# Moving three pieces of hand-ordered work in an attention and feed-forward kernel: key differences, output products, first row maxima

## The chip, the cores and the metric

The kernel runs on one core of a Trainium2 chip. The metric is the device time of one execution in microseconds; lower is better. The profile is one execution, taken by the hardware profiler; its engines are PE (matrix multiply; PEld is its weight load), DVE (VectorE), ACT (ScalarE), POOL (GpSimd) and SP (SyncE, which here only issues transfers).

## The reference

A transformer block on one sequence of 2048 rows of 576 numbers: a layer norm, attention with 32 heads of 18 numbers, an output product with a residual, a second layer norm, and a gated feed-forward part with 4608 inner columns.

```python
x = A_x                                                   # 1 x 2048 x 576
h = x + _A_ref(_layernorm(x), A_wqkv, A_wo)
h2 = h + _B_ref(_layernorm(h), B_w_gate, B_w_up, B_w_down)

def _A_ref(x, wqkv, wo):                                  # 32 heads, Dh = 18
    q, k, v = split(x @ wqkv)
    p = softmax(einsum("bhqd,bhkd->bhqk", q, k) * Dh ** -0.5)
    return einsum("bhqk,bhkd->bhqd", p, v) @ wo

def _B_ref(x, w_gate, w_up, w_down):
    return (gelu(x @ w_gate) * (x @ w_up)) @ w_down
```

## The kernel before

Products of float32 precision are made from pairs of float16 numbers (a high and a low part), so every product is three matmuls.

**Stages.** First come the layer norm and the products for q, k and v; then the attention loop; then the feed-forward part.

**The attention loop** runs over 32 blocks `n`. A block is one group of four heads (`g = n // 4`) and 512 queries (`qc = n % 4`), and walks over 16 key tiles `kt` of 128 keys. For each key tile PE makes four score tiles of 128 keys by 512 queries (`score`, line 670), ACT takes their exponentials (line 672), and PE weighs the values with them (`weigh`, line 679, one key tile later).

**Row maxima run ahead.** Before a block's scores can be made, the largest score of each query must be known; it is subtracted inside the score product, as two extra rows of the stacked queries. PE makes the scores once more for this (`max_bank`, line 618) and DVE reduces each bank (line 629), 64 banks to a block, some 1.45 blocks ahead: 93 banks are made before the loop, eight for every two key tiles in it. `max_finish` ends a block: DVE takes the last maximum (line 638), POOL splits it into float16 parts (lines 641 to 643), SP turns them (`mT`, line 645) and issues four transfers that put them into the stacked queries (line 651, tiles `A` or `W`). So the last maximum is made in block 30, key tile 8.

**Key differences.** A quarter of the banks for maxima use differences of neighbouring key stretches in place of keys. `load_ends` (line 591) loads keys, `key_steps` has POOL subtract them (lines 598 to 601), and SP writes them to DRAM (`kd`, line 604) and reads them back (line 606). It is done once for each group of heads after the first, a group ahead: in block 1 and in blocks 4, 8, 12, 16, 20 and 24.

**Out-block.** When a block has been weighed, `out_block` works in three steps in the next block: the sums are taken from the banks, added on POOL (line 696), and their denominators fetched (`rc`, line 701); the reciprocals are made on POOL (lines 708 to 712; on DVE, line 714, for the last four blocks) and spread over the partitions through DRAM (lines 716 and 717); and `o` is scaled (line 721 on POOL, 725 on DVE for the last two), split, and written into the stack `X` (lines 736 to 740).

**Output product.** `wo_block(b)` multiplies four row tiles of `o` by `wo` (PE line 301, 14 matmuls to a half tile; eight half tiles to a block of rows), adds the residual (DVE line 809), and takes the statistics of the second layer norm; POOL makes their roots in pairs of tiles (`rstd_beside`, line 226 on). Rows of block `b` need `o` of all heads, that is, of the last group. `rows0` then norms the first 1024 rows in pairs (tile `i` and tile `4 + i`), makes sums of them on POOL (lines 850 to 853) and float16 parts on DVE (lines 859 to 863), and SP turns them into the layout of the feed-forward products (line 889). The feed-forward part begins when PE comes to line 1135.

**What sets the order.** PE, ACT, DVE and POOL execute what the code issues, in that order. Inside the attention loop the order on SP is chosen by the scheduler, which may move a transfer ahead of others whose data are later; every engine and queue then works strictly in its order. `take(it)` advances a piece of work by one step, and the steps of a key tile stand in `STEPS`: `s` a score tile, `m` a bank for maxima, `w` half a key tile weighed, `f` other work, where `side` is the splitting of the first weights on POOL.

Of the kernel before, what the change touches and what calls it, by code (L numbers as in the profile page):

```python
# [26 lines left out]
HALF = D // 2  # L27
# [5 lines left out]
def tile_block(  # L33
# [18 lines left out]
    nc = tc.nc  # L52
# [4 lines left out]
    NT = S // P  # L57
    TB = min(512, S)
    NB = S // TB
    TPB = TB // P  # L60
# [5 lines left out]
    NG = H // 4  # L66
# [13 lines left out]
    def ring(items):  # L80
        while True:
            yield from items

    p_ring = ring(quads)
    m_ring = ring(singles)
    

    nat = const.tile([P, NT, D], F32, name="nat")
# [97 lines left out]
    def row_stats(src, t):  # L186
        st = small.tile([P, 2, 6], F32, tag="st", name="st", bufs=4)
        for i in range(2):
            nc.vector.bn_stats(st[:, i], src[:, i * HALF : (i + 1) * HALF])
        nc.vector.bn_aggr(mv[:, t], st)  # L190
# [26 lines left out]
    minus_half = const.tile([P, 1], F32, name="minus_half")  # L217
    nc.gpsimd.memset(minus_half, -0.5)

    def rstd_beside(t0, nt, scale):  # L220

        sl = slice(t0, t0 + nt)
        v = small.tile([P, nt], F32, tag="ln_v", name="ln_v")
        r = small.tile([P, nt], F32, tag="ln_r", name="ln_r")
        u = small.tile([P, nt], F32, tag="ln_u", name="ln_u")
        nc.gpsimd.tensor_scalar_add(v, mv[:, sl, 1], EPS)
        nc.gpsimd.tensor_tensor(r, v, minus_half.to_broadcast([P, nt]), op=ALU.pow)
        for k in (1.0, scale):
            nc.gpsimd.tensor_mul(u, r, r)
            nc.gpsimd.tensor_mul(u, u, v)  # L230
            nc.gpsimd.tensor_scalar(u, u, -0.5 * k, 1.5 * k, op0=ALU.mult, op1=ALU.add)
            nc.gpsimd.tensor_mul(r if k == 1.0 else rs[:, sl], u, r)
        nc.gpsimd.tensor_mul(u, mv[:, sl, 0], rs[:, sl])
        nc.gpsimd.tensor_scalar_mul(nb[:, sl], u, -1.0)
# [79 lines left out]
    def take(it, n=1):  # L314
        for _ in range(n):
            next(it, None)
# [4 lines left out]
    xv = x.rearrange("(t p) d -> p t d", p=P)  # L321
# [422 lines left out]
    NS = NG * NB  # L744
    UPS = TPB * NB
    AHEAD = UPS + 8 * UPS // 16
# [19 lines left out]
    u_o = const.tile([P, 1], F32, name="u_o")  # L766
# [25 lines left out]
    xbs = [view(A, MAT, (D,)), view(WK, 19968, (D,))]  # L792
    PIECES = 2 * NK + 9

    def wo_block(b, ring_, xbs=xbs):

        def fetch(t):
            if t < (b + 1) * TPB:
                nc.sync.dma_start(xbs[t % 2], xv[:, t])

        fetch(b * TPB)
        fetch(b * TPB + 1)
        yield
        for t in range(b * TPB, (b + 1) * TPB):
            for i in range(2):
                ws = slice(i * HALF, (i + 1) * HALF)
                pt = next(ring_)
                run(accumulate(pt[:, :HALF], products(slice(t * P, (t + 1) * P), oh, ol, ws)))
                nc.vector.scalar_tensor_tensor(nat[:, t, ws], pt[:, :HALF], u_o, xbs[t % 2][:, ws],
                                               op0=ALU.mult, op1=ALU.add)  # L810
                yield
            fetch(t + 2)
            row_stats(nat[:, t], t)
            if t % 2:
                rstd_beside(t - 1, 2, 256.0)
        yield


    VP = view(V, 0, (2 * PIECES, TB), F16)
# [10 lines left out]
    def rows0():  # L830

        o = 2 * PIECES * TB
        parts = [(view(r, k, (4, 5 * P), F16), view(V, o + 8064 + 5120, (2, 5 * P), F16),
                  view(V, o + 8064 + 7680, (1, 5 * P), F16))
                 for r, k in ((V, o + 8064), (tmp3.rearrange("p a b -> p (a b)"), 0))]
        r12 = view(V, o + 8064 + 5120, (3, 5 * P), F16)
        bufs = [(view(V, o, (7, HALF)), T4s),
                (view(nat1, 18432, (7, HALF)), view(nat1, 18432 + 4 * 7 * HALF, (HALF,)))]
        M2, M3 = 2 * P, 3 * P
        for rows in (parts[0][0], parts[1][0], r12):  # L840
            nc.gpsimd.memset(rows[:, :, M3 - KR : M3], 0.0)

        def sums(i):
            F, T4 = bufs[i % 2]
            b12, B22, B11, B21, T1, T2, T3 = (F[:, k] for k in range(7))
            y2, y1 = (F.rearrange("p a b -> p (a b)")[:, k * D : (k + 1) * D] for k in range(2))
            normed(y1, nat[:, i], i)
            normed(y2, nat[:, TPB + i], TPB + i)
            yield
            nc.gpsimd.tensor_sub(T1, b12, B11)  # L850
            nc.gpsimd.tensor_sub(T2, B22, T1)
            nc.gpsimd.tensor_sub(T4, B21, T2)
            nc.gpsimd.tensor_sub(T3, B22, b12)
            yield

        def cut_rows(i):
            F, T4 = bufs[i % 2]
            for k, (f, r) in enumerate(zip((F[:, 1:5], F[:, 5:7], T4.unsqueeze(1)), parts[i % 2])):
                nc.vector.tensor_copy(r[:, :, :HALF], f)
                yield  # L860
                nc.vector.tensor_sub(r[:, :, M3:], f[:, :, :M2], r[:, :, :M2])
                nc.vector.tensor_sub(r[:, :, HALF : HALF + KR], f[:, :, M2:], r[:, :, M2:HALF])
                nc.vector.tensor_copy(r[:, :, HALF + KR : HALF + 2 * KR], r[:, :, M2:HALF])
                if k == 0:
                    turn_rows(0, i, 0, 20, r)
                elif k == 2:
                    turn_rows(0, i, 20, 35, r12)
                yield

        yield from sums(0)  # L870
        for i in range(TPB):
            if i + 1 < TPB:
                yield from sums(i + 1)
            yield from cut_rows(i)
# [63 lines left out]
    B22, B11, B21, T1, T2, T3, T4 = range(7)  # L938
# [306 lines left out]
    mxs = maxima()  # L1245
# [9 lines left out]
    fill = other_products()  # L1255
    side = iter(())
    take(fill, 18)
    for i in range(5 * AHEAD // 4):
        take(mxs, 1 if i == 5 * AHEAD // 4 - 1 else 3 + (i % 5 == 4))
        if i == AHEAD // 4:  # L1260
            raw_loads()
        if i >= AHEAD // 3:
            take(sums)
        take(fill, 2 + (i % 5 == 2))
    run(sums)
    m_ring = ring(singles[:3] + quads[:3])
    accs = (singles[3], quads[3])
    STEPS = ("smsmwsmsf", "wsmssmmwsmmwf")
    halves = deque([None, None])
    for n in range(NS):  # L1270
        g, qc = divmod(n, NB)
        late = n > NS - NB
        for kt in range(NT):
            heads = iter(range(4))
            for step in STEPS[kt % 2]:
                if step == "s":
                    score(n, kt, next(heads))
                elif step == "m":
                    take(mxs)
                elif step == "w":  # L1280
                    half_ = halves.popleft()
                    if half_ is not None:
                        weigh(*half_)
                        if half_[1] == NT - 1 and half_[3] == 1:
                            ob = out_block(half_[0], accs)
                            next(ob)
                else:
                    if n < NS - 1 or kt < 11:
                        take(fill, 2)
                    take(side)  # L1290
            halves += [(n, kt, accs, q) for q in range(2)]
            if n and kt in ((2 if n == NS - 1 else 4, 7) if late else (4, 6)):
                take(ob)
            if late and kt == 11:
                run(fill)
                fill = wo_block(qc - 1, m_ring)
                take(fill, qc == 3)
            if n == NS - 2 and kt == NT - 1:
                rows = rows0()
            if n * NT + kt >= (NS - 1) * NT - 1:  # L1300
                take(rows, 2)
            if g == 0 and qc == 0 and kt == NT - 1:
                run(fill)
                init_set(sets[1])
            if g + 1 < NG and kt == 2 and qc == (1 if g == 0 and NB > 1 else 0):
                load_stacks(g + 1)
                load_ends(g + 1)
            if g + 1 < NG and kt == 8 and qc == (1 if g == 0 and NB > 1 else 0):
                key_steps(g + 1)
            if n == 2 and kt == 4:  # L1310
                side = prepare_wo()
            if n == NS - NB and kt == 2:
                blank_rows()
                load_matrix(w_gate, 0, nc.gpsimd)
            if n == NS - NB and kt == 8:
                side = chain(split_early(0, 0, lambda: load_matrix(w_up, 0, nc.gpsimd)), pause(2),
                             split_early(0, 1, lambda: load_matrix(w_gate, 1, nc.gpsimd)),
                             pause(2), until_ready(second))
# [18 lines left out]
    m_ring = ring([singles[3], more[3]])  # L1337
# [27 lines left out]
    rows = chain(rows1(), first_load())  # L1365
# [63 lines left out]
```

## Time and profile before

| | |
|---|---|
| median of 3 runs | 2678.67 us (2677.91 to 2679.49) |
| profiled execution | 2680.21 us |
| its span | 2678.4 us |
| PE busy | 2591.2 us (97%) |
| DVE busy | 2003.9 us (75%) |
| ACT busy | 1666.6 us (62%) |
| POOL busy | 856.7 us (32%) |
| mean granted PE clock | 0.985 |
| attention loop, about | 204 to 1455 us |
| feed-forward part, from | 1469.66 us |

The busy shares are means over stages with different limits. In the attention loop ACT, DVE and PE are all nearly full; in the feed-forward part PE alone is. Times of rows are microseconds from the start of the span. A row of the timeline has start, duration, engine, line and operation, and in brackets how long the engine was idle before it and what ended that. A row of the waits has the total, the number of waits, and the longest.

### The profile page before, as it was taken

What the parts mean: (1) busy time and instruction counts of PE and PEld (TensorE: products, weight loads), DVE (VectorE), ACT (ScalarE), POOL (GpSimd) and SP (SyncE); (2) the same over time, 40 slices, a digit from 0 to 9 for tenths busy, and PEclk for the clock granted to TensorE, in tenths of its full rate; (3) what the DMA queues carried; (4) which work ended last, traced back from release to release, by engine and by line L of the source; (5) the groups of instructions that cost most, each with busy time, mean ns of one, the idle gap of its engine ahead of it and who ended that gap; (6) DMA issues with size and microseconds to landing.
All of it is one profiled execution on the core that took longest, in us unless ns stands there. A gap on an engine that the chain in (4) does not pass through costs nothing.

```text
span 2678.4 us, 96899 instructions
## 1 busy us (share of the span) xinstructions
PE 2591.2 (97%) x41245; PEld 1495.0 (56%) x41245; DVE 2003.9 (75%) x3888; ACT 1666.6 (62%) x3154; POOL 856.7 (32%) x1176
## 2 busy tenths in 40 slices
PE   8999899989998999999989999999999999999999
PEld 4545555555555555555555555555555555555555
DVE  7479889989898999989856766565656566666653
ACT  6229889989898999989955533333333333333332
POOL 4302532322323232332755632222222222222221
PEclk9999999999999999999989999999999999999999
DMA  8621010101101010100115331010101010101010
GB/s 221 149 83 39 18 48 19 42 18 32 35 18 42 18 47 20 42 17 22 39 39 104 88 67 40 22 40 23 40 23 40 23 40 22 40 25 38 27 60 36
DMA packets 170372, 121.00 MB, mean 45 GB/s; under 512 B 88665, under 2 KB 147565, under 8 KB 169939
## 3 DMA queue, kind: packets, MB, share of 16 engines
q1 hardware_dynamic: 161198, 98.47, 13.7%
q0 software_dynamic: 8608, 16.33, 2.4%
q8 instruction: 322, 5.28, 0.8%
q14 instruction: 112, 0.91, 0.1%
q10 hardware_dynamic: 132, 0.01, 0.0%
HBM read 80.05 MB, written 15.01 MB: 35 GB/s over the span
## 4 chain that ended last, share of the span: by engine, by line
PE 78%; POOL 6%; DMA 4%; DVE 4%; issue 3%; SPq 3%; ACT 1%; POOLq 0%; DVEq 0%; ACTq 0%
PE bank L1135 14%; PE more L1135 14%; PE bank L301 10%; PE more L301 8%; PE quad L679 6%; PE bank L679 5%; PE quad L618 5%; PE bank L618 5%; PE quad L301 4%; PE bank L670 4%; PE quad L670 3%; DVE mx L629 2%; SPq L604 1%; POOL rp L708 1%; DMA A<-qk_hi 1%
## 5 line engine op out<-in xcount | busy, mean ns | idle before, releaser
L672 ACT ACTIVATE WK<-bank 128x512 f32<-128x512 f32 x1109 | 726.3, 750 | 70.7 <-PE bank L618 27.5
L679 PE MATMUL bank<-WK,V 64*32 64x256 f32 x8192 | 660.1, 385 | 2.2 <-ACT nat L693 0.3
L672 ACT ACTIVATE WK<-quad 128x512 f32<-128x512 f32 x939 | 638.5, 747 | 28.8 <-PE quad L618 21.8
L679 PE MATMUL quad<-WK,V 64*32 64x256 f32 x8192 | 647.0, 384 | 1.9 <-DVE nat L698 1.7
L629 DVE TENSOR_REDUCE mx<-quad 128x1 f32<-128x512 f32 x813 | 542.2, 683 | 46.3 <-PE quad L618 40.5
L629 DVE TENSOR_REDUCE mx<-bank 128x1 f32<-128x512 f32 x739 | 493.4, 683 | 54.1 <-PE bank L618 43.4
L1135 PEld LDWEIGHTS <-W 128*128 128x128 f16 x2394 | 234.0, 98 | 278.6 <-issue 0.2
L301 PEld LDWEIGHTS <-WK 128*128 128x128 f16 x3456 | 338.2, 98 | 88.3
L679 PEld LDWEIGHTS bank<-WK,V 64*32 64x32 f32 x8192 | 238.6, 107 | 35.6 <-ACT WK L672 12.4
L679 PEld LDWEIGHTS quad<-WK,V 64*32 64x32 f32 x8192 | 226.7, 106 | 18.1 <-DVE nat L698 2.2
L301 PE MATMUL more<-W,WK 128*128 128x288 f16 x1728 | 235.2, 286 | 0.0
L301 PE MATMUL bank<-W,WK 128*128 128x288 f16 x1728 | 235.2, 286 | 0.0
L670 PEld LDWEIGHTS <-A 56*32 56x32 f16 x4096 | 149.0, 92 | 145.6 <-issue 58.9
L1135 PE MATMUL bank<-X,W 128*128 128x512 f16 x792 | 223.8, 379 | 0.0
L670 PE MATMUL bank<-A 56*32 56x512 f16 x2220 | 207.6, 386 | 14.2 <-DMA A<-mT 13.3
L670 PE MATMUL bank<-W 56*32 56x512 f16 x2216 | 207.0, 389 | 12.9 <-DMA W<-mT 12.4
L670 PEld LDWEIGHTS <-W 56*32 56x32 f16 x4096 | 146.3, 92 | 128.5 <-issue 53.5
L1135 PE MATMUL bank<-V,W 128*128 128x512 f16 x720 | 202.4, 379 | 0.0
L1003 POOL TENSOR_TENSOR A<-A 128x384 f32<-128x384 f32 x136 | 137.7, 1033 | 201.5 <-ACT tmp L1140 82.8
L618 PE MATMUL quad<-W 54*32 54x512 f16 x2040 | 199.0, 386 | 1.5 <-DVE mx L629 0.6
L618 PEld LDWEIGHTS <-W 54*32 54x32 f16 x4096 | 132.5, 90 | 110.7 <-issue 96.9
L670 PE MATMUL quad<-A 56*32 56x512 f16 x1876 | 173.9, 384 | 16.1 <-DMA A<-mT 14.9
(352 smaller groups left out, 4560.4 us busy)
## 6 DMA issues: line engine op xcount, KB each, us to landing
A<-in_B_w_down_dram SPq DMA_DIRECT2D x8, 1152.0 KB
nat<-rc SPq DMA_DIRECT2D x32, 256.0 KB
A<-in_B_w_gate_dram SPq DMA_DIRECT2D x64, 128.0 KB
A<-in_B_w_up_dram SPq DMA_DIRECT2D x64, 128.0 KB
qk_hi<-tmp SPq DMA_DIRECT2D x36, 128.0 KB
qk_lo<-tmp SPq DMA_DIRECT2D x36, 128.0 KB
out_dram<-nat SPq DMA_DIRECT2D x16, 288.0 KB
X<-nat SPq DMA_DIRECT2D x100, 36.0 KB
```

The source lines that it names most:

```text
L301: nc.tensor.matmul(dst, a, b, start=(i == 0), stop=(i == len(pairs) - 1))
L604: nc.sync.dma_start(k[:, :, s], d[s * DH : (s + 1) * DH])
L618: nc.tensor.matmul(pm[c : c + CT, :TB], Q[r, q0 + c : q0 + c + CT], keys, start=True, stop=True)
L629: nc.vector.tensor_reduce(dst, pm[:, :TB], axis=AX.X, op=ALU.max)
L670: nc.tensor.matmul(pS[c : c + CT, :TB], K[r, kt * P + c : kt * P + c + CT], Q[r, qc * TB : (qc + 1) * TB], start=True, stop=True)
L672: nc.scalar.activation(pes[(2 * kt + hh // 2) % NPE][:, hh % 2], pS[:, :TB], AF.Exp, scale=ex_reg)
L679: nc.tensor.matmul(acc[CT * hh : CT * hh + CT, qs], Vg[n // NB][ks, kt * G4 + hh * VC : kt * G4 + hh * VC + CT], pes[(2 * kt + hh // 2) % ...
L708: nc.gpsimd.tensor_tensor(rc[:, c : c + 4], den[:, c : c + 4], minus_one.to_broadcast([P, 4]), op=ALU.pow)
L1003: op(W8[:, d], W8[:, a], W8[:, b])
L1135: nc.tensor.matmul(bank, w, x_, start=start and i == 0, stop=i == len(mm) - 1, skip_group_check=not start)
```

## The change

It does four things.

1. `key_steps` is called at key tile 12 instead of 8, so that it stands behind `max_finish` (key tile 9) in the program.
2. The second and third steps of `out_block` come at key tiles 3 and 5 instead of 4 and 6; in blocks 29 and 30 at 3 and 6 instead of 4 and 7; in the last block at 2 and 6 instead of 2 and 7.
3. `wo_block(0)` and `wo_block(1)`, which ran in blocks 29 and 30 from key tile 11 on, two half tiles to a key tile, become `wo_pairs`: tiles 0, 4, 1, 5, 2, 6, 3, 7, one half tile to a key tile, four key tiles out of five, from the key tile after the last maximum on (block 30, key tile 9). `rows0` starts in the last block at key tile 4 instead of 15, and its two buffers are swapped. One half tile of `wo_block(2)` moves from behind the loop into its last key tile.
4. Before the loop, the 93 first banks for maxima are made in 23 bursts of four and one single bank, instead of 24 bursts of three, five of four and a single one.

The diff, without the lines that only rename an index:

```diff
-    def rstd_beside(t0, nt, scale):
-        sl = slice(t0, t0 + nt)
+    def rstd_beside(t0, nt, scale, by=1):
+        sl = slice(t0, t0 + (nt - 1) * by + 1, by)
...
-    def wo_block(b, ring_, xbs=xbs):
+    def wo_tiles(ts, ring_, xbs=xbs):
+        by = ts[1] - ts[0]
+        def fetch(k):
+            if k < len(ts):
+                nc.sync.dma_start(xbs[k % 2], xv[:, ts[k]])
+        fetch(0)
+        fetch(1)
+        yield
+        for k, t in enumerate(ts):
             for i in range(2):
...
+                if i == 1:
+                    fetch(k + 2)
+                    row_stats(nat[:, t], t)
+                    if k % 2:
+                        rstd_beside(t - by, 2, 256.0, by)
                 yield
+    def wo_block(b, ring_, xbs=xbs):
+        return wo_tiles(list(range(b * TPB, (b + 1) * TPB)), ring_, xbs)
+    def wo_pairs(ring_):
+        return wo_tiles([t for i in range(TPB) for t in (i, TPB + i)], ring_)
...
-            F, T4 = bufs[i % 2]
+            F, T4 = bufs[(i + 1) % 2]
...
-        take(mxs, 1 if i == 5 * AHEAD // 4 - 1 else 3 + (i % 5 == 4))
+        take(mxs, 0 if i % 5 == 4 else 1 if i == 5 * AHEAD // 4 - 2 else 4)
...
+    LAST_MAX = (NS - 1) * NT - 7
+    rows = rows0()
...
-                    if n < NS - 1 or kt < 11:
-                        take(fill, 2)
                     take(side)
...
-            if n and kt in ((2 if n == NS - 1 else 4, 7) if late else (4, 6)):
+            if n and kt in ((2 if n == NS - 1 else 3, 6) if late else (3, 5)):
                 take(ob)
-            if late and kt == 11:
+            if n * NT + kt == LAST_MAX - 2:
+                fill = wo_pairs(m_ring)
+                take(fill)
+            after = n * NT + kt - LAST_MAX
+            if after >= 0 and after % 5 < 4:
+                take(fill)
+            if after >= 11:
+                take(rows, 2)
+            if n == NS - 1 and kt == NT - 2:
                 run(fill)
-                fill = wo_block(qc - 1, m_ring)
-                take(fill, qc == 3)
-            if n == NS - 2 and kt == NT - 1:
-                rows = rows0()
-            if n * NT + kt >= (NS - 1) * NT - 1:
-                take(rows, 2)
+                fill = wo_block(2, m_ring)
+                take(fill)
...
-            if g + 1 < NG and kt == 8 and qc == (1 if g == 0 and NB > 1 else 0):
+            if g + 1 < NG and kt == 12 and qc == (1 if g == 0 and NB > 1 else 0):
                 key_steps(g + 1)
```

**On SP, in block 1** (the same happens in blocks 4 to 24). `kd` are the differences on their way to DRAM, `mT` the turned maxima, `X` the stack that takes `o`, `rc` the denominators of the next out-block. Before:

```order
L736 DMA X<-nat 18x2x512 x4
L604 DMA kd_856<-nat 36x1x128 x4
L604 DMA kd_857<-nat 36x1x128 x4
L606 DMA nat<-kd_856 18x1024 x2
L645 DMA_TRANSPOSE mT<-mm_858 128x1x128
L591 DMA nat<-qk_hi 18x4x128
L606 DMA nat<-kd_857 18x1024
L591 DMA nat<-qk_hi 18x4x128
L651 DMA A<-mT 2x4x128 x4
L591 DMA nat<-qk_hi 18x4x128
L591 DMA nat<-qk_lo 18x4x128 x3
L701 DMA rc<-nat 128x1x16
```

After:

```order
L736 DMA X<-nat 18x2x512 x4
L645 DMA_TRANSPOSE mT<-mm_858 128x1x128
L591 DMA nat<-qk_hi 18x4x128 x2
L604 DMA kd_856<-nat 36x1x128
L651 DMA A<-mT 2x4x128 x4
L604 DMA kd_856<-nat 36x1x128 x3
L604 DMA kd_857<-nat 36x1x128 x4
L606 DMA nat<-kd_856 18x1024 x2
L591 DMA nat<-qk_hi 18x4x128
L606 DMA nat<-kd_857 18x1024
L591 DMA nat<-qk_lo 18x4x128 x3
L701 DMA rc<-nat 128x1x16
```

The turn of the maxima and the four transfers of them stood behind eleven transfers of differences; now the turn stands ahead of all of these, and the four transfers behind one. All that was ahead of them is now between them and the next `rc`.

**On POOL, in block 30.** Lines 1065 to 1069 (after: 1075 to 1079) split the first weights, lines 721 to 723 scale and split `o` of block 29, lines 987 and 989 (997 and 999) are loads of weights, line 641 is the maximum of block 31. Before:

```order
L1065 TENSOR_SCALAR A<-A,p_s_m_30894 128x768
L1066 CAST W<-A 128x768
L721 TENSOR_TENSOR nat<-nat 128x512
L722 CAST nat<-nat 128x512
L723 TENSOR_TENSOR nat<-nat 128x512
L1068 TENSOR_TENSOR WK<-A,W 128x512
L1069 TENSOR_TENSOR W<-A,W 32x2x128
L641 TENSOR_SCALAR m<-m 128x16
```

After:

```order
L1078 TENSOR_TENSOR WK<-A,W 128x256
L1079 TENSOR_TENSOR W<-A,W 32x128
L721 TENSOR_TENSOR nat<-nat 128x512
L722 CAST nat<-nat 128x512
L723 TENSOR_TENSOR nat<-nat 128x512
L997 DMA A<-in_B_w_gate_dram 128x2x128
L999 DMA A<-in_B_w_gate_dram 96x1x128
```

The scaling of `o` has moved ahead of the eight loads of weights and of the piece of splitting that followed them.

**On DVE, around the end of `rows0`** (before) and at its start (after). Lines 809 and 811 are the same statement, the residual of the output product; lines 859 to 863 and 869 to 873 are the same, the parts of `rows0`. Before:

```order
L859 CAST V<-nat 128x288
L861 TENSOR_TENSOR V<-nat,V 128x256
L862 TENSOR_TENSOR V<-nat,V 128x32
L863 COPY V<-V 128x32
L698 TENSOR_TENSOR nat<-quad_76,nat 128x512
L809 SCALAR_TENSOR_TENSOR nat<-quad_75,u_o,A 128x288
L809 SCALAR_TENSOR_TENSOR nat<-bank_66,u_o,A 128x288
```

After:

```order
L811 SCALAR_TENSOR_TENSOR nat<-bank_66,u_o,WK 128x288
L189 BN_STATS st<-nat 128x6 x2
L190 BN_AGGR mv<-st 128x2
L869 CAST V<-nat 128x4x288
L871 TENSOR_TENSOR V<-nat,V 128x4x256
L872 TENSOR_TENSOR V<-nat,V 128x4x32
L873 COPY V<-V 128x4x32
L869 CAST V<-nat 128x2x288
L871 TENSOR_TENSOR V<-nat,V 128x2x256
L872 TENSOR_TENSOR V<-nat,V 128x2x32
L873 COPY V<-V 128x2x32
L811 SCALAR_TENSOR_TENSOR nat<-quad_73,u_o,A 128x288
```

All parts of the four pairs of rows stood ahead of the residuals of the third block of rows; now parts of rows and residuals alternate.

More of the change, by code (lines that the diff above doesn't have):

```diff
@@ L793, in tile_block @@
     PIECES = 2 * NK + 9
-    def wo_block(b, ring_, xbs=xbs):
[L797 to L802, printed above, removed]
+    def wo_tiles(ts, ring_, xbs=xbs):
[5 more added lines that the diff above has]
+        fetch(1)
         yield
-        for t in range(b * TPB, (b + 1) * TPB):
+        for k, t in enumerate(ts):
             for i in range(2):
@@ L808, in wo_block @@
                 run(accumulate(pt[:, :HALF], products(slice(t * P, (t + 1) * P), oh, ol, ws)))
-                nc.vector.scalar_tensor_tensor(nat[:, t, ws], pt[:, :HALF], u_o, xbs[t % 2][:, ws],
+                nc.vector.scalar_tensor_tensor(nat[:, t, ws], pt[:, :HALF], u_o, xbs[k % 2][:, ws],
                                                op0=ALU.mult, op1=ALU.add)
-                yield
[L812 to L816, printed above, removed]
+                if i == 1:
[3 more added lines that the diff above has]
+                        rstd_beside(t - by, 2, 256.0, by)
+                yield
+    def wo_block(b, ring_, xbs=xbs):
+        return wo_tiles(list(range(b * TPB, (b + 1) * TPB)), ring_, xbs)
+    def wo_pairs(ring_):
+        return wo_tiles([t for i in range(TPB) for t in (i, TPB + i)], ring_)
     VP = view(V, 0, (2 * PIECES, TB), F16)
@@ L856, in cut_rows @@
         def cut_rows(i):
-            F, T4 = bufs[i % 2]
+            F, T4 = bufs[(i + 1) % 2]
             for k, (f, r) in enumerate(zip((F[:, 1:5], F[:, 5:7], T4.unsqueeze(1)), parts[i % 2])):
```

## The prediction

> **What bounds the kernel now.** I read the page, then busy time by stretch, the waits on the tile that the first edit moves, and the queues around one such wait. Two blocks of the attention loop, one in which key differences are made and the next (stretch, its length, busy PE, PEld, DVE, ACT, POOL, granted clock, DMA):
>
> ```profile
> span 2678.4 us, 96899 instructions
> ...
> 512.80:557.60 44.80, 37.52 (x1027) 21.26 (x1015) 35.22 (x67) 36.37 (x74) 18.63 (x32) 0.89 0.20 49
> 557.60:593.80 36.20, 35.96 (x1048) 20.92 (x1037) 35.38 (x67) 35.91 (x74) 9.69 (x16) 1.00 0.06 17
> ```
>
> ACT does the same work in both, 36 us, and fills the ordinary block; in the other some 9 us are nobody's. Those who waited for `mT`, all blocks, and the wait of this block:
>
> ```profile
>   PE bank L670: 25.7, 4
>   PE quad L670: 21.4, 3
> PE bank L670 <- DMA A<-mT: 7.1, 1, 7.1
> ```
>
> PE waits seven times, 47.1 us in all, and there are seven blocks with key differences. SP's queue in this block, then in ordinary ones, and first and last start of the 28 out-blocks 0 to 27:
>
> ```profile
> 512.76 0.62 SPq L701 DMA_DIRECT2D rc<-nat  x1
> ...
> 534.69 3.92 SPq L736 DMA_DIRECT2D X<-nat  x5
> 538.71 6.51 SPq L604 DMA_DIRECT2D kd<-nat  x8
> ...
> 546.15 1.15 SPq L645 DMA_TRANSPOSE mT<-mm  x1
> ...
> 549.57 2.75 SPq L651 DMA_DIRECT2D A<-mT  x4
> ...
> 553.22 2.73 SPq L591 DMA_DIRECT2D nat<-qk_lo  x3
> 557.63 0.64 SPq L701 DMA_DIRECT2D rc<-nat  x1
> ...
> 593.77 0.60 SPq L701 DMA_DIRECT2D rc<-nat  x1
> ...
> 614.22 1.12 SPq L645 DMA_TRANSPOSE mT<-mm  x1
> 616.46 2.06 SPq L651 DMA_DIRECT2D A<-mT  x3
> ...
> 629.66 0.60 SPq L701 DMA_DIRECT2D rc<-nat  x1
> ...
> 245.16 0.61 SPq L701 DMA_DIRECT2D rc<-nat  x1
> 1271.51 0.60 SPq L701 DMA_DIRECT2D rc<-nat  x1
> ```
>
> `rc` opens each block, so its distance is the period: 35.89 us ordinarily (593.77 to 629.66), 44.87 here. Over 27 periods, 1271.51 - 245.16 - 27 x 35.89 = 57.3 us too much, 8.2 to each of the seven. The turn of the maxima comes 33.4 us after `rc` here and 20.45 ordinarily. What held it is ahead of it on SP: eight `kd` writes, which waited for POOL:
>
> ```profile
> 533.50 1.16 POOL L723 TENSOR_TENSOR nat<-nat 128x512 f16<-128x512 f32 x1
> 534.62 1.29 POOL L598 TENSOR_TENSOR nat<-nat 72x256 f32<-72x256 f16 x2
> ...
> 537.25 0.67 POOL L601 TENSOR_TENSOR nat<-nat 72x256 f16<-72x256 f32 x1
> ...
> 538.61 0.22 POOL L643 TENSOR_TENSOR mm<-m,mm 128x16 f16<-128x16 f32 x1
> ```
>
> **Part one: differences later.** POOL makes the maximum's parts straight after line 723, 3.3 us sooner (534.62 to 537.92), then the differences. SP then turns at 538.7 (it still issues `X` until 538.61), issues two loads of 0.91 (2.73 / 3) and one `kd` of 0.81 (6.51 / 8), and the transfers of `mT` begin at 538.7 + 1.15 + 1.82 + 0.81 = 542.5 and not 549.57: 7.1 sooner. Those loads and that `kd` wait for the differences, which are done by 534.66 + 0.85 + 3.3 = 538.8, earlier than SP reaches them. The first of these transfers landed here at
>
> ```profile
> 550.33 1.70 DMA A<-mT
> ```
>
> 552.03, 2.46 after the start of its issue, so PE wanted it at 552.03 - 7.1 = 544.9, or `rc` + 32.2. Now it lands at 545.0. The wait goes, with nothing to spare.
>
> What is late next: all that stood ahead of `mT` now stands between it and the next `rc`: 542.5 + 2.75, seven `kd` (5.7), three reads back (about 1.1), four loads (3.6) end at 555.6, while the next block begins at 512.76 + 35.89 = 548.65. So `rc` is some 7 us late, and POOL's reciprocals, the scaling of `o` and, behind it, the next maximum with it. That block's transfers of `mT` began 22.69 after its start and land at 25.15, against 32.2: a margin of 7.05, just used up. I leave 0.7 us to each of seven for such remainders: 57.3 - 5 = 52 us.
>
> The clock: the stalled block ran at 0.89 of it, the other at 1.00, and 57.3 - 47.1 = 10.2 us of the excess is not waiting itself. The Trainium skill (TensorE: Matmul & The Clock Gate, What's actually happening) has the clock halve after an idle window of about 3.4 us; waits of 6 to 8 us and the granted clock agree, and by it remainders under that cost no clock. If any wait did, 10 us less would come back, and the time were 2615.
>
> The earlier steps of the out-block move nothing on POOL here, since its next instruction there is the same; they act only in the late blocks.
>
> **Part two: the end of attention.** Out-block 28 opens block 29 at 1307.86. From there to the first matmul of the feed-forward part:
>
> ```profile
> 1307.86 0.60 SPq L701 DMA_DIRECT2D rc<-nat  x1
> ...
> 1331.48 1.28 PE L301 MATMUL quad<-W,X 128*128 128x288 f16 x9
> 1336.04 0.90 PE L301 MATMUL quad<-W,X 128*128 128x288 f16 x3 [3.28 <-DMA X<-nat]
> ...
> 1394.01 0.87 PE L301 MATMUL quad<-W,X 128*128 128x288 f16 x3 [2.07 <-DMA X<-nat]
> 1398.71 0.64 PE L301 MATMUL quad<-W,X 128*128 128x288 f16 x2 [3.83 <-DMA X<-nat]
> ...
> 1403.07 4.20 PE L301 MATMUL quad<-W,X 128*128 128x288 f16 x28
> 1408.19 3.60 PE L301 MATMUL quad<-W,X 128*128 128x288 f16 x28
> 1413.79 3.60 PE L301 MATMUL quad<-W,X 128*128 128x288 f16 x28
> ...
> 1455.65 1.89 PE L301 MATMUL quad<-W,X 128*128 128x288 f16 x14
> ...
> 1469.66 1.67 PE L1135 MATMUL more<-X,A 128*128 128x512 f16 x7
> ...
> 1430.00:1440.00 10.00, 10.00 (x245) 5.22 (x244) 4.49 (x6) 9.97 (x21) 8.00 (x9) 1.00 1.08 147
> ```
>
> 161.8 us. Prices: a half tile is (1469.66 - 1455.65) / 8 = 1.75. A key tile with maxima is 35.89 / 16 = 2.24; without them 4 x 9.97 / 21 = 1.90, ACT full. Two key tiles with two halves each took 1413.79 - 1403.07 = 10.72, so the rest of one is 1.86 and a key tile with one half 3.61: PE sets it.
>
> By these, before, from 3.7 into block 29 (35.89 - 32.2): 25 key tiles with maxima 56.1, eight halves in them 14.0, three with two halves 16.1, two with one 7.2, 18 without 34.2, and behind the loop eight halves and the last weighing (1, an estimate from 1.86) 15: 142.6 - 3.7 = 138.9. The other 22.9 us are waits, the two seen first of all: PE stands in the output product for `X`, at 1332 and 1392, with scores and maxima queued behind it, and restarts slowly.
>
> After: 25 with maxima 56.1, 17 with one half 61.4, six without 11.4, seven halves and the weighing 13.3, less 3.7: 138.5. The work is the same; the 22.9 us are at stake. The first wait goes: `o` of block 28 has a whole block more. For the second, POOL scales `o` of block 29 ahead of eight weight loads and a split piece, and PE needs it at the third half tile: I keep 2 us. `mT` of block 30 stands behind POOL's splitting, 1 to 2 us late. Together 4 us: 19 gained. The normed rows move under the last block's scores, where DVE has only residuals; the feed-forward part then begins when PE is through, as before.
>
> **Part three: bursts.** PE is never idle there; three banks and four cost it the same (chain of waits):
>
> ```profile
> 105.77 0.56 PE bank L618 x12
> ...
> 113.75 0.57 PE bank L618 x16
> ```
>
> Six bursts fewer: 6 x 0.56 = 3.4; DVE must empty four banks before the next burst, so I take 3.
>
> **Sum:** 52 + 19 + 3 = 74 from the profiled execution's 2680.21: 2606.2. The median of the runs is 1.54 lower: 2604.7, rounded to 2605.
>
> **Rivals.**
> - *SP gives the wait back one block on.* The margin of 7.05 is used up on paper. If SP's loads and reads back take 3 us longer, six following blocks wait 3 us and lose 1.4 of clock: 26 us, 2631. For it: seven counts of 0.8 us in one queue. Against: the count is of rows.
> - *DVE gives the end back.* Parts of rows now stand between residuals, and a cast waits for a transfer of the rows before it:
>
> ```profile
> 1460.20 0.46 DVE L859 CAST V<-nat 128x576 f16<-128x576 f32 x1 [3.24 <-DMA V<-V]
> ...
> 1424.48 1.23 DVE L861 TENSOR_TENSOR V<-V 128x1024 f16<-128x1024 f32 x1
> ...
> 1431.87 1.70 DVE L861 TENSOR_TENSOR tmp<-nat,tmp 128x1024 f16<-128x1024 f32 x1
> ```
>
>   Six such waits of 3.24 while PE's banks fill up cost 19 us: 2624. Against: a pair of rows now has four key tiles, some 13 us.
> - *The differences don't get out of the way*, as POOL obeys no key tile: then 52 is lost, 2657. The order speaks against it.
> - *Slower:* on SP the transfers of `mT` still stand behind one `kd`. Were POOL's differences held, say behind the next out-block's sums, `mT` would wait for them. Gain turns into loss when these transfers start later than before by (19 + 3) / 7 = 3.1 us, at `rc` + 39.9; the differences would have to end some 13 us after the 538.8 counted. At `rc` + 42 it were 2693. On POOL they stand ahead of those sums.
>
> **How the numbers follow.** Forecast 0.66 (2590 to 2615: the remainders of both parts, 5 and 4 us, gone or twice as large, and 5 less if PE needs less beside a half tile than 1.86), SP 0.13, DVE 0.14, no move 0.03, slower 0.03, unnamed 0.01. The range 2590 to 2630 holds the first, DVE, and the milder half of SP: 0.85. A measurement tells 0.2% (5 us) from no change: faster 0.95, within 0.02, slower 0.03.
>
> **What would show it.** Right: periods of 36 us throughout, no PE wait on `mT` over 2 us; `kd` behind `mT` on SP, `rc` some 7 us late in the blocks after; output products from block 30's key tile 9 on, no long wait for `X`; the first matmul of line 1145 (1135 now) near 1395. Wrong: new waits on `mT` in blocks 2, 5, 9 and so on, or DVE residuals late and PE idle in block 31.

## The result, and the profile after

The changed kernel takes 2630.3 us (median of four runs, 2626.11 to 2634.42) against 2678.64: a ratio of 0.9819, with a 95% interval of 0.9802 to 0.9836. The forecast was 2605. So 48 us came and 74 were announced; the time lies just outside the range of 2590 to 2630. The profiled execution took 2630.88 us, its span 2629.1.

Where the 49.3 us of span came from is read off the start of each block's `rc` on SP and the first feed-forward matmul. First, twenty-eighth and twenty-ninth `rc` (SP's timeline, after):

```profile
245.56 0.61 SPq L701 DMA_DIRECT2D rc<-nat  x1
...
1238.76 0.60 SPq L701 DMA_DIRECT2D rc<-nat  x1
...
1275.12 0.60 SPq L701 DMA_DIRECT2D rc<-nat  x1
```

| stretch | before | after | gained | forecast |
|---|---|---|---|---|
| start to the first `rc` (bursts) | 245.2 | 245.6 | -0.4 | 3 |
| 27 periods (key differences) | 1026.4 | 993.2 | 33.2 | 52 |
| `rc` of block 28 to that of block 29 | 36.4 | 36.4 | 0 | 0 |
| from there to the feed-forward part | 161.8 | 142.8 | 19.0 | 19 |
| feed-forward part to the end | 1208.7 | 1211.2 | -2.5 | 0 |

The end of attention gave what was forecast, the bursts nothing, and the key differences two thirds.

**Where the rest of the periods went.** SP's queue in the block that the prediction showed, and in the next (start and length in us, line, form, tile, count):

```profile
508.02 0.62 SPq L701 DMA_DIRECT2D rc<-nat  x1
...
538.08 2.74 SPq L651 DMA_DIRECT2D A<-mT  x4
540.86 6.14 SPq L604 DMA_DIRECT2D kd<-nat  x7
547.17 1.54 SPq L606 DMA_DIRECT2D nat<-kd  x2
548.76 0.79 SPq L591 DMA_DIRECT2D nat<-qk_hi  x1
549.73 0.36 SPq L606 DMA_DIRECT2D nat<-kd  x1
550.13 2.35 SPq L591 DMA_DIRECT2D nat<-qk_lo  x3
552.59 0.64 SPq L701 DMA_DIRECT2D rc<-nat  x1
559.46 0.35 SPq L716 DMA_DIRECT2D rc<-rp  x1
561.96 0.59 SPq L717 DMA_DIRECT2D nat<-rc  x1
...
576.11 2.75 SPq L651 DMA_DIRECT2D A<-mT  x4
...
583.69 0.60 SPq L701 DMA_DIRECT2D rc<-nat  x1
```

The block's own transfers of `mT` now start 30.06 us after its `rc` and no longer 36.81, and its wait of 7.1 us is down to 0.8, nearly as forecast. But what was ahead of them now stands ahead of the next `rc`. POOL had the sums ready at

```profile
543.72 1.28 POOL L696 TENSOR_TENSOR nat<-nat 128x512 f32<-128x512 f32 x1 [9.33 <-DVE nat L695]
```

543.72 + 1.28 = 545.0; SP copies them at 552.59, 7.6 us later. Against a period of 35.89 from 508.02 the copy is 8.68 us late, and in that block the transfers of `mT` start 576.11 - 552.59 = 23.52 after it: 32.20 in all. Behind blocks 4, 12 and 20 the copy is only 7.1, 6.6 and 6.7 us late, but the transfers start 24.9 to 25.4 after it. There the reciprocals' way through DRAM, from the issue of line 716 to that of line 717, takes 3.3 to 3.6 us; in the kernel before it took 1.4 to 1.8 in the same blocks (SP, changed kernel, block 13):

```profile
697.89 0.64 SPq L701 DMA_DIRECT2D rc<-nat  x1
704.76 0.35 SPq L716 DMA_DIRECT2D rc<-rp  x1
708.16 0.59 SPq L717 DMA_DIRECT2D nat<-rc  x1
```

PE now waits above all in the blocks *after* those with differences (waits for `mT`, blocks 1 to 28):

```profile
PE bank L670 <- DMA A<-mT: 9.8, 8, 5.4
PE bank L670 <- DMA W<-mT: 5.4, 3, 2.6
PE quad L670 <- DMA W<-mT: 2.7, 2, 2.4
PE quad L670 <- DMA A<-mT: 1.2, 2, 0.9
```

19.1 us in place of 47.1: 16.8 in the blocks after, 2.2 in blocks 1, 8 and 16 themselves. Over a block with differences and the next together, the excess above 2 x 35.89 is 9.7, 4.2, 3.9, 3.5, 3.1, 3.8 and -0.2 us for blocks 1, 4, 8, 12, 16, 20 and 24. Block 24 is the only one behind which no group's `ends` are left to load: its next `rc` is only 3.9 us late, and nobody waits. Block 1 has a cause of its own. In block 2 POOL also prepares the output matrix (lines 779 to 782), and the rest of one column's work and the whole of the next slip in between the scaling of `o` and the maximum's parts:

```profile
306.52 1.16 POOL L723 TENSOR_TENSOR nat<-nat 128x512 f16<-128x512 f32 x1
307.63 0.66 POOL L781 CAST W<-nat 128x576 f16<-128x576 f32 x1
...
313.55 0.25 POOL L641 TENSOR_SCALAR m<-m 128x16 f32<-128x16 f32 x1
```

Six us there, on a block whose `rc` was late already: this is the wait of 5.4.

**The end.** No wait for `X` is left. PE ends its last output product, stands idle, and starts the feed-forward part slowly; SP meanwhile stood at the transposes of the normed rows, with an `x` row behind them that the last residual needs (PE's and SP's timelines, then the wait and the clock):

```profile
1411.75 1.88 PE L301 MATMUL bank<-W,X 128*128 128x288 f16 x14
1417.93 3.15 PE L1145 MATMUL more<-X,A 128*128 128x512 f16 x7 [4.30 <-DVE nat L811]
```

```profile
1412.47 1.25 SPq L899 DMA_TRANSPOSE V<-tmp  x1
1413.82 0.53 SPq L801 DMA_DIRECT2D WK<-in_A_x_dram  x1
```

```profile
1413.82 3.46 DMA WK<-in_A_x_dram
```

```profile
1417.93:1420.43 2.50, 2.50 (x6) 0.86 (x6) 1.43 (x5) 0.00 (x0) 0.93 (x2) 0.50 0.30 61
1420.43:1422.93 2.50, 2.50 (x7) 0.91 (x6) 0.00 (x0) 1.69 (x2) 1.74 (x9) 0.50 0.02 3
```

The chain of what ended last goes through that `x` row (3.46 us from issue). For 5 us after it the granted clock is 0.50: at half speed that loses 2.5 us, by which the feed-forward part is longer.

### The profile page after: what moved, and what is told of

Its sections match the earlier page's. It is cut to its first block, busy times and chain, and to the rows that moved or that the text cites. A ratio compares the mean times of both kernels' runs of the same rounds, so it can differ in the third digit from the quotient of the medians.

```text
span 2629.1 us, 96913 instructions
## 1 busy us (share of the span) xinstructions
PE 2578.3 (98%) x41245; PEld 1490.7 (57%) x41245; DVE 2007.7 (76%) x3888; ACT 1667.6 (63%) x3154; POOL 854.2 (32%) x1176
## 4 chain that ended last, share of the span: by engine, by line
PE 77%; POOL 6%; issue 4%; SPq 4%; DVE 4%; DMA 3%; ACT 1%; POOLq 0%; DVEq 0%; ACTq 0%
PE bank L1145 15%; PE more L1145 15%; PE bank L301 11%; PE more L301 8%; PE quad L679 5%; PE bank L679 5%; PE quad L618 4%; PE bank L618 4%; PE quad L301 4%; PE bank L670 3%; PE quad L670 3%; DVE mx L629 2%; POOL rp L708 2%; SPq L604 1%; SPq L591 1%
## 5 line engine op out<-in xcount | busy, mean ns | idle before, releaser
L672 ACT ACTIVATE WK<-quad 128x512 f32<-128x512 f32 x946 | 648.9, 756 | 19.1 <-PE quad L670 9.3
L679 PE MATMUL bank<-WK,V 64*32 64x256 f32 x8192 | 645.4, 382 | 2.4 <-ACT nat L693 0.3
L629 DVE TENSOR_REDUCE mx<-quad 128x1 f32<-128x512 f32 x815 | 544.2, 684 | 16.8 <-PE quad L618 11.1
L679 PEld LDWEIGHTS bank<-WK,V 64*32 64x32 f32 x8192 | 231.2, 106 | 24.4 <-ACT nat L693 11.1
L679 PEld LDWEIGHTS quad<-WK,V 64*32 64x32 f32 x8192 | 226.0, 106 | 16.8 <-issue 1.0
L670 PEld LDWEIGHTS <-W 56*32 56x32 f16 x4096 | 143.7, 91 | 120.9 <-issue 52.3
L618 PEld LDWEIGHTS <-A 54*32 54x32 f16 x4096 | 124.9, 90 | 113.7 <-issue 98.9
```

The lines of the kernel that those rows point to most:

```text
L618: nc.tensor.matmul(pm[c : c + CT, :TB], Q[r, q0 + c : q0 + c + CT], keys, start=True, stop=True)
L629: nc.vector.tensor_reduce(dst, pm[:, :TB], axis=AX.X, op=ALU.max)
L670: nc.tensor.matmul(pS[c : c + CT, :TB], K[r, kt * P + c : kt * P + c + CT], Q[r, qc * TB : (qc + 1) * TB], start=True, stop=True)
L672: nc.scalar.activation(pes[(2 * kt + hh // 2) % NPE][:, hh % 2], pS[:, :TB], AF.Exp, scale=ex_reg)
L679: nc.tensor.matmul(acc[CT * hh : CT * hh + CT, qs], Vg[n // NB][ks, kt * G4 + hh * VC : kt * G4 + hh * VC + CT], pes[(2 * kt + hh // 2) % ...
```

## The experiments

Theory: SP's queue gives a part of the wait back one block on; what counts is when a block's transfers of `mT` start, and as long as they start within about 30 us of the time at which the block should have begun, nobody waits. Rivals are named with each run. "Stretch" is the time from the first to the twenty-eighth `rc`, read as above.

| run | time, us | ratio to before, 95% interval | stretch, us |
|---|---|---|---|
| the change | 2630.3 | 0.9819 (0.9802 to 0.9836) | 993.2 |
| key differences alone | 2643.7 | 0.9869 (0.9852 to 0.9885) | 990.0 |
| without the key differences | 2660.4 | 0.9938 (0.9921 to 0.9954) | 1022.3 |
| writes and reads on POOL | 2610.6 | 0.9752 (0.9736 to 0.9768) | 974.3 |
| output matrix prepared later | 2624.4 | 0.9803 (0.9787 to 0.9819) | 987.1 |
| bursts undone | 2626.8 | 0.9807 (0.9789 to 0.9825) | 989.3 |
| two writes for eight | 2606.0 | 0.9733 (0.9717 to 0.9749) | 967.6 |
| x rows on ACT | 2621.7 | 0.9792 (0.9772 to 0.9812) | 989.1 |
| all transfers of differences on POOL | 2645.8 | 0.9886 (0.9870 to 0.9903) | 1006.3 |
| stacks later | 2617.0 | 0.9768 (0.9753 to 0.9783) | 982.0 |
| before, with stacks later | 2694.3 | 1.0064 (1.0049 to 1.0079) | 1040.0 |
| four edits together | 2601.6 | 0.9713 (0.9700 to 0.9726) | 966.7 |

Where the stretch should read as in the change (bursts undone, x rows, the key differences alone) it reads 989 to 993: one profile of it is good to some 4 us. Beside these runs the kernel before took 2676.3 to 2677.9 us.

**The parts by themselves.** On the kernel before, the key differences alone:

```diff
-            if g + 1 < NG and kt == 8 and qc == (1 if g == 0 and NB > 1 else 0):
+            if g + 1 < NG and kt == 12 and qc == (1 if g == 0 and NB > 1 else 0):
                 key_steps(g + 1)
```

> The kernel before with one edit: key differences at key tile 12 instead of 8. Theory (SP gives a part of the wait back): in the changed kernel the stretch from the first to the twenty-eighth out-block got 33.2 us shorter, not the 52 of the prediction, and this edit is the only one that acts there; so 2678.6 - 33 = 2646, and periods with key differences that together with the next still hold about 4 us too much in five groups, about 10 in the first and none in the last. Rival (the other edits cost something in this stretch, such as the earlier steps of the out-block): 2627, with 52 us gained and the two-block excess under 1 us.

34 us gained, and the same excesses group by group (7.4, 4.6, 3.8, 3.3, 3.3, 3.3, -0.2). The loss is in this edit alone; the rest of the change costs nothing in the stretch that these 4 us would show. The changed kernel without it (12 back to 8):

> The changed kernel with the key differences back at key tile 8; the end of attention and the bursts stay changed. Theory: the end gives 19.0 us from the out-block of block 29 to the feed-forward part, which then runs 2.5 us longer, and the bursts nothing: 2678.6 - 16.5 = 2662, with the stretch of 28 out-blocks at 1026 us as before. Rival (the edits interact: the earlier steps of the out-block help or hurt the stalled blocks): the stretch differs from 1026 us by more than 3.

17.5 us gained; from the `rc` of block 29 to the feed-forward part 143.7. The stretch is 4 us shorter than before, one more than the theory allowed, and no more than it varies between runs. 34.2 + 17.5 = 51.7 against 48.3 for the whole: the parts add up within their intervals.

**Is it SP's queue?** In the changed kernel POOL issues the writes and reads:

```diff
-                nc.sync.dma_start(k[:, :, s], d[s * DH : (s + 1) * DH])
+                nc.gpsimd.dma_start(k[:, :, s], d[s * DH : (s + 1) * DH])
...
-            nc.sync.dma_start(steps[g % 2][i * DH : (i + 1) * DH],
+            nc.gpsimd.dma_start(steps[g % 2][i * DH : (i + 1) * DH],
```

> The changed kernel with the eight writes of the differences and the three reads back issued by POOL and no longer by SP. Theory (SP's queue makes the next block's sums late): without the eleven transfers, 8.4 us of SP, the four loads of ends are issued by 544 in the block that starts at 508, the copy of the sums goes out when POOL has it (545.0 there, and not 552.6), and the next maximum is in time. Of the 28 us left in the first 28 blocks the five later groups lose about 3.7 each and the first some 3: 2630 - 21 = 2609. Rival one (POOL becomes late instead: it waits for the writes before it can issue the reads, and its sums of the next block stand behind them): no gain, 2630, or a loss if POOL is late by more than the 7.6 us of now. Rival two (what is left has nothing to do with SP's queue): 2630.

2610.6: 20 us regained with eleven issues taken off SP, and the waits fall to 4.5 us. The stretch of 974.3 is what the prediction had forecast. The excesses are 0.4, -0.1, 2.4, 0.3, 4.8, -0.2, -0.2: what is left is in blocks 8 and 16, where five transfers of `X` and not four stand on SP ahead of those of `mT`, beside three loads of `ends` as in blocks 1, 12 and 20 too (SP, block 16, whose `rc` was at 784.58):

```profile
811.75 1.86 SPq L645 DMA_TRANSPOSE mT<-mm  x1
813.66 2.34 SPq L591 DMA_DIRECT2D nat<-qk_hi  x3
816.11 2.75 SPq L651 DMA_DIRECT2D A<-mT  x4
```

They start 31.5 after `rc` here and 30.5 in block 8, in the five others at 27.7 to 29.4, where the latest, block 12, waits 0.3: the limit is close to 29.4. The number of issues can also be cut on SP itself:

```diff
-    kd = [dram.tile([DH, HB, DQ, DI], F16, name=f"kd{i}") for i in range(2)]
+    kd = [dram.tile([DQ * DH, HB, DI], F16, name=f"kd{i}") for i in range(2)]
...
-            for s in range(DQ):
-                nc.sync.dma_start(k[:, :, s], d[s * DH : (s + 1) * DH])
+            nc.sync.dma_start(k, d)
...
-            nc.sync.dma_start(steps[g % 2][i * DH : (i + 1) * DH],
-                              k.rearrange("r h s i -> r h (s i)"))
+            nc.sync.dma_start(steps[g % 2][i * DH : (i + 1) * DH].rearrange("r h (s i) -> r h s i", s=DQ),
+                              k.rearrange("(s r) h i -> r h s i", s=DQ))
```

> The changed kernel with two writes of the differences in place of eight (the buffer in memory is laid out by quarters, and the three reads back put them in order), all still on SP. Six issues fewer, 4.7 us: the copy of the sums in the next block goes out some 2.9 us late and no longer 7.6. Theory (a margin: a block bears its sums some 5 us late for nothing): nearly all is gained that POOL's issue gained, 19 of 20 us: 2611. Rival (each microsecond of lateness is paid): 4.7 / 8.4 of it, 11 us: 2619. If reads of 256-byte pieces take longer, the steps come later, which nobody waits for.

2606.0, 24 us better than the change and 5 better than forecast. `rc` is still late behind these blocks, by 1.6 to 4.6 us, and of all the waits for `mT` one of 0.3 us is left:

```profile
PE bank L669 <- DMA A<-mT: 0.3, 1, 0.3
```

So lateness is not paid by the microsecond: 4.6 us cost nothing, 6.6 to 8.7 in the changed kernel cost three to four. The margin of the prediction exists. The reciprocals' way through DRAM is shorter here too, 1.4 to 2.4 us in the blocks behind; how much of the gain is due to it and how much to the earlier copy is not told apart.

**The first group.**

```diff
-            if n == 2 and kt == 4:
+            if n == 6 and kt == 4:
                 side = prepare_wo()
```

> The changed kernel with the output matrix prepared on POOL from block 6 on and no longer from block 2. Theory: in block 2 a piece of this work, 3.7 us, stands on POOL between the scaling of o and the maximum's parts, where the sums are late already; the first group's two blocks hold 9.7 us too much against about 3.9 in the groups of blocks 4 to 20. Moved to block 6, which no group touches, the first group falls to about 4: 2630 - 6 = 2624. Rival (the first group is long for another reason, such as the stacks of the second group, which are loaded in the same block): no change, or the same 3.7 us show in block 6 or 7 again.

The first group falls from 9.7 to 3.0, nothing shows in blocks 6 and 7, and the stretch is 6.1 us shorter. The time fell by 6 too, though its interval overlaps that of the change.

**What else makes a block late: POOL.** All transfers of the differences on POOL, `ends` included, with the two writes of above and the x rows of below:

```diff
-                nc.sync.dma_start(
-                    e[s * DH : (s + 1) * DH],
+                nc.gpsimd.dma_start(
+                    e[s * DH : (s + 1) * DH],
```

> The changed kernel with all transfers of the differences on POOL: two writes in place of eight, three reads, and the eight loads of ends; and with the last x rows on ACT. Theory: where only the writes and reads were on POOL, the first 28 blocks kept 5.3 us too much, nearly all in blocks 8 and 16, where three loads of ends stand on SP ahead of the transfers of the maxima; without them the stretch is 27 x 35.89 = 969 us, 24 us less than 993.2, and the feed-forward part gains what the x rows alone gain, 6: 2630 - 30 = 2600. Rival (four to eight loads more on POOL, 0.5 us each, make its sums late in the next block): the stretch stays at 974 or longer, and the time at 2605 or above.

A miss, 46 us above the theory: 2645.8, slower than the change. Nothing is late in the next block; the block itself is. The eight loads now stand on POOL ahead of the reciprocals (block 8, `rc` at 503.38; POOL, SP, and PE's wait):

```profile
514.37 2.30 POOL L591 DMA_DIRECT2D nat<-qk_lo  x4
516.69 3.99 POOL L707 TENSOR_TENSOR rp<-rc,minus_one 128x4 f32<-128x4 f32 x4
```

```profile
537.89 0.67 SPq L650 DMA_DIRECT2D A<-mT  x1
```

```profile
PE bank L669 <- DMA A<-mT: 4.9, 1, 4.9
```

Reciprocals start 13.3 us after `rc`, in the changed kernel 7.3, in an ordinary block 2.0; the transfers of `mT` start at 34.5 and not 30.1, and PE waits 4.9. I had weighed POOL's queue for the next block and not for this one. It suggests that the changed kernel's own block had no slack either, because of the twelve stack transfers that POOL issues there first. So, in the changed kernel, those later:

```diff
-            if g + 1 < NG and kt == 2 and qc == (1 if g == 0 and NB > 1 else 0):
+            if g + 1 < NG and kt == 10 and qc == (1 if g == 0 and NB > 1 else 0):
                 load_stacks(g + 1)
                 load_ends(g + 1)
```

> The changed kernel with the next group's stacks (twelve issues on POOL, twelve on SP) started at key tile 10 and no longer at 2, so that on POOL they stand behind the maximum's parts and not ahead of the reciprocals. Theory (in the block that makes differences everything is late because POOL starts its reciprocals 7.3 us after the sums' copy and not 2.0): the transfers of the maximum start near 22.5 us into that block, as in an ordinary one, the differences' writes near 30, and the sums of the next block are some 5 us late, which with 22.7 more is under the 29.9 at which PE begins to wait. The stretch of 28 out-blocks becomes 970 us, 23 less, with SP issuing as many transfers as now: 2607. Rival (the lateness comes from the number of transfers on SP alone): nothing is gained, 2630.

2617.0: 13 us gained of the 23 expected, between theory and rival. Block 8, `rc` at 501.49:

```profile
522.25 1.18 SPq L645 DMA_TRANSPOSE mT<-mm  x1
527.83 2.71 SPq L651 DMA_DIRECT2D A<-mT  x4
530.65 1.65 SPq L591 DMA_DIRECT2D nat<-qk_hi  x2
532.41 6.49 SPq L604 DMA_DIRECT2D kd<-nat  x8
...
544.70 0.64 SPq L701 DMA_DIRECT2D rc<-nat  x1
```

The maximum turns at 20.8, but its transfers start 5.6 us after the turn began and not 2.3, while the twelve stacks that POOL has just issued move, so at 26.3; the writes begin at 30.9, as counted, and end late enough to put the next `rc` 7.3 us behind and not 5. So POOL's late start was a part of the loss. The copy is still late behind SP's queue, and in block 9 the reciprocals' way through DRAM still takes 3.07 us; the shares of these two were not separated. The same edit on the kernel before, with differences still at key tile 8:

> The kernel before with one edit: stacks at key tile 10 in place of 2; differences stay at key tile 8. POOL then makes its reciprocals and the differences 5 us sooner, but on SP the maximum's turn now stands behind eight writes, three reads and eight loads of ends. Theory (what stands ahead on SP sets it): X ends near 19 us into the block, eight writes 6.5, reads with their wait 4, eight loads 6.5, so the turn comes at 36 and its transfers near 38.5, against 36.8 in the kernel before: each of seven blocks waits some 2 us longer, 2678 + 13 = 2691. Rival (POOL's late start was what set it): seven waits fall by 5 us and more: 2640 or less.

Slower, as the count of SP's queue has it: 2694.3 against 2691, the stretch 13.7 us longer against 13. Block 8, `rc` at 517.26, and the largest group of PE's waits, two of 9:

```profile
538.02 6.63 SPq L604 DMA_DIRECT2D kd<-nat  x8
...
550.09 3.09 SPq L591 DMA_DIRECT2D nat<-qk_lo  x4
553.29 1.15 SPq L645 DMA_TRANSPOSE mT<-mm  x1
555.55 2.78 SPq L651 DMA_DIRECT2D A<-mT  x4
```

```profile
PE bank L670 <- DMA A<-mT: 18.1, 2, 9.5
```

POOL is 5 us sooner here, and the transfers start at 38.3 all the same. What stands ahead on SP decides, as in the slower rival.

**Bursts and the end.** First maxima as before the change:

```diff
-        take(mxs, 0 if i % 5 == 4 else 1 if i == 5 * AHEAD // 4 - 2 else 4)
+        take(mxs, 1 if i == 5 * AHEAD // 4 - 1 else 3 + (i % 5 == 4))
```

> The changed kernel with the first maxima in threes and fours again, as before the change. Theory (what six bursts fewer save, 3.4 us, comes back as PE's waits for banks that DVE has not emptied, 3.2 us of idle PE from 100 to 180 us against 1.0, and as a clock of 0.96 to 0.98 from 180 to 246 against 1.00): the first out-block starts within 1 us of 245.6, PE is busy all but 1 us of 100 to 180, and the time is 2630 within 2. Rival (the bursts do save 3 us, and something else in the changed kernel costs it): the first out-block starts 3 us later, near 248.6, and the time is 2633.

The first `rc` is at 245.35 against 245.56, and the time does not differ beyond its interval. Over all kernels the first `rc` starts at 245.4 us on average with the new bursts (nine profiles, 244.4 to 246.9) and at 245.6 with the old (four, 245.2 to 246.4). PE from 100 to 180 us, in the changed kernel, in this one, and in the kernel before:

```profile
100.00:180.00 80.00, 76.78 (x706) 39.74 (x704) 61.61 (x109) 18.21 (x49) 13.03 (x22) 1.00 0.40 104
```

```profile
100.00:180.00 80.00, 78.61 (x706) 39.03 (x703) 60.89 (x106) 18.03 (x47) 13.02 (x22) 1.00 0.40 105
```

```profile
100.00:180.00 80.00, 79.02 (x698) 39.78 (x696) 60.58 (x106) 18.49 (x49) 13.04 (x22) 1.00 0.39 105
```

PE has 1.8 to 2.2 us less work there and as much more idle time, part of it seen as waits of 1.4 and 0.6 us for DVE's maxima. The clock half of my theory fell: from 180 to 246 us it is 0.97 with the old bursts too (1.00 in the kernel before).

The x rows of the last output products from ACT's queue:

```diff
-                nc.sync.dma_start(xbs[k % 2], xv[:, ts[k]])
+                (nc.sync if k < 2 else late).dma_start(xbs[k % 2], xv[:, ts[k]])
...
-                fill = wo_block(2, m_ring)
+                fill = wo_block(2, m_ring, late=nc.scalar)
```

> The changed kernel with the two x rows that the last block of output products still fetches issued by ACT and no longer by SP, where they stand behind the transposes of the normed rows. Theory (in the changed kernel the last residual waits 2.6 us for such a row, PE stands idle 4.3 us ahead of the feed-forward part, whose first matmuls then take 3.15 and 2.48 us in place of 1.5): the feed-forward part begins 4 us sooner after the out-block of block 29 (139 and not 142.8) and runs 2.5 us shorter (1208.7): 2630 - 6 = 2624. Rival (PE waits for the last normed rows just behind, so the row only uncovers them): 2630, with PE idle as long and the wait now for the transposes.

PE's idle time falls from 4.3 to 2.0, and the feed-forward part begins 140.5 us after the `rc` of block 29, 2.3 sooner; it runs 0.6 shorter, not 2.5. The rest of the wait is now for POOL, which was late with statistics (line 233). So 3 us of the 6.7 in the span are shown; the other 4 are in the stretch, where the edit can't act. The interval of the time overlaps that of the change.

**Together.** Two writes, stacks at key tile 10, output matrix from block 6, x rows on ACT:

> The changed kernel with four edits together: two writes of the differences in place of eight, stacks at key tile 10, the output matrix prepared from block 6 on, the last x rows on ACT. Theory: fewer writes alone left 967.6 us for the stretch of 28 out-blocks, so nothing is left there but 1 to 2 us, and the x rows give 3 us at the end: 2606 - 5 = 2601. Rival (the first two edits each take away the same lateness and the others are hidden): 2606, within 2.

2601.6, as forecast: 76 us under the kernel before and 29 under the change, with an interval clear of both. It overlaps that of two writes alone, so what the other three edits add is not shown by the times. In the profiles the end, from the `rc` of block 29 on, is 3.2 us shorter than with two writes alone, as the 3 us of the theory, and the stretch 0.9. No wait for `mT` is left in the stretch, and its 966.65 us are 27 periods of 35.80.

## Why the prediction was right and wrong

- *The stalled blocks' own wait goes, with nothing to spare:* right but for 0.8 us of 7.1 in block 8. The transfers start at 30.06 against the 29.74 worked out.
- *"I leave 0.7 us to each of seven for such remainders":* this step failed. By the prediction's own count 57.3 - 33.2 = 24.1 us were left, 3.4 to each and not 0.7 (28 in the two-block excesses, since the other periods are a little under 35.89). It set a lateness of 7 us equal to a margin of 7.05, let the block behind run from its late copy as an ordinary one does, and then treated the case as nearly free. Both terms were too small. Behind block 8 the next `rc` was 8.7 us late, since the queue behind the transfers took 14.5 us (538.08 to 552.59) and not 13.1 and began 0.3 later; and in the next block the transfers start 23.52 after `rc` and not 22.69. Together that is 2.46 us over the margin; PE waited 0.8 us for block 8's own transfers and 2.0 for the next. Behind blocks 4, 12 and 20 the lateness was as counted, 6.6 to 7.1, and the transfers started 24.9 to 25.4 after `rc`, because of the reciprocals' longer way through DRAM; PE waited 2.4 to 3.0. The rival *SP gives the wait back* had the lateness that becomes a wait one block on, 3 us in place of 1.3 to 3.0, and 2631: it is what happened, in five blocks and with a sixth of its own kind, though the longer way through DRAM was not in it. It deserved the larger chance, since in every block two numbers met with no room between.
- *Block 2:* not seen at all. The output matrix's work on POOL was under the wait before; it was worth 6 us once the block was late.
- *No clock lost in waits under 3.4 us:* failed. The 27 periods exceed 27 x 35.80 by 26.5 us, and waits are 19.1. The other 7.4 are put down to the clock, which was 0.90 to 0.95 in blocks 2, 5, 9, 13 and 21 and 1.00 in the rest (below). The rival had counted 1.4 us a wait for it.
- *The end:* right in size, 142.8 against 142.5 (138.5 and 4 of waits), but in part by luck. The waits for `X` are gone, and the 2 us kept for one of them weren't needed; `mT` of block 30 was 1.6 us late, as counted. All waits of PE there come to 7.6 us and not 4, the rest to 135.2 and not 138.5: two errors that nearly cancel. *"The feed-forward part then begins when PE is through, as before"* failed: 4.3 us idle behind an `x` row, counted at nothing, and a clock that cost 2.5 more. DVE, the rival, held PE for 0.9 us there.
- *Bursts, 3 us:* failed. The 2 us of work saved became idle time of PE, a part of it as waits for DVE's maxima; what ended the rest of it is not shown.

## What to carry to other kernels

When a queue's work is moved behind an urgent transfer, it stands ahead of the next urgent one: write down how late that becomes and how late it may be, and if the two numbers meet, forecast the wait and not its absence. Fewer issues on the queue were worth more than another order of them, and another engine's queue helped only as long as nothing urgent stood behind them there. A wait that goes uncovers what it hid: here POOL's work on the output matrix and an `x` row behind transposes.

## What the runs showed of the hardware

**Short waits can cost clock.** Behind the wait of 1.7 us in block 9 the granted clock fell, and behind one of 1.0 us in block 17 it did not (changed kernel, 2.5 us stretches from the end of the wait; the clock stands ahead of the DMA share):

```profile
577.90:580.40 2.50, 2.15 (x55) 0.82 (x63) 1.84 (x4) 1.79 (x3) 0.00 (x0) 0.89 0.05 12
580.40:582.90 2.50, 2.50 (x56) 1.42 (x46) 1.58 (x4) 2.16 (x5) 0.51 (x1) 0.50 0.00 0
582.90:585.40 2.50, 2.50 (x80) 1.61 (x68) 2.50 (x5) 2.10 (x6) 0.77 (x1) 0.93 0.03 3
```

```profile
871.84:874.34 2.50, 2.09 (x56) 0.87 (x64) 1.83 (x4) 1.78 (x3) 0.00 (x0) 1.00 0.03 9
874.34:876.84 2.50, 2.42 (x79) 1.23 (x65) 2.18 (x5) 2.39 (x6) 1.09 (x1) 1.00 0.00 0
```

The three stretches of block 9 lack 0.68 x 2.5 = 1.7 us of clock, on a wait of 1.7. In the changed kernel the waits of 1.7, 2.4, 2.4, 2.6 and 5.4 us were all followed by a stretch at 0.50, those of 0.5, 0.9, 1.0 and, in block 29, 1.6 by none; with the x rows on ACT, the idle 2.0 us ahead of the feed-forward part were followed by 5 us at 0.70 and 0.62. Over the timelines of all thirteen profiles, from the first `rc` to the feed-forward part, no wait of 0.8 to 1.1 us was followed by such a fall (but for two of 0.9 us, 0.4 apart); of the 33 between 1.2 and 2.0 us 25 were; and of those over 2.0 us all but one, of 2.4. What decides between 1.2 and 2.0 us was not tried. The Trainium skill (TensorE: Matmul & The Clock Gate, What's actually happening) has the clock fall after an idle window of about 3.4 us; here a third to a half of that was often followed by the same fall.

**A transfer takes longer behind others.** The reciprocals' way through DRAM took 2.4 to 3.6 us in the changed kernel's six blocks behind a queue of writes, reads and loads that made the sums late, and 1.43 to 1.48 in the same blocks of the kernel of the four edits; the turn of the maxima took 5.6 us and not 2.3 while twelve stacks moved. That the shared transfer engines are the reason was not tried.
